# Agent attention and a leaky MLP on one core: scores in two column tiles, another spread of the second batch's side work, another order of loads

## The chip, the core and the metric

The kernel runs on one core of a Trainium2 chip. The metric is the device time of one execution in microseconds (us); three runs of the kernel before took 1022.23, 1023.3 and 1019.7 us, median 1022.23. A separate execution was profiled; its own time is 1020.48 us. Rows of the trace come from that one.

The engines are TensorE (PE in the rows; its weight loads are PEld), VectorE (DVE), ScalarE (ACT), GpSimd (POOL) and SyncE (SP), which issues the loads and stores. Each works through its own instructions in the order in which the program gives them, and waits on semaphores for the others. Products land in PSUM, from which VectorE and ScalarE read.

## The reference

Two batches of 12480 queries, keys and values of 128 channels, and 49 agents per batch. The agents attend to the keys, the queries attend to the agents, and the result goes through a two-layer MLP with a leaky ReLU.

```python
def _attn_ref(q, k, v, agents):
    scale = 1.0 / np.sqrt(q.shape[-1])
    def sm(a, b):
        s = scale * (a @ b.transpose(0, 2, 1))
        s = s - s.max(-1, keepdims=True)
        e = np.exp(s)
        return e / (e.sum(-1, keepdims=True) + 1e-09)
    agent_v = sm(agents, k) @ v
    return (sm(q, agents) @ agent_v).astype(np.float32)

def _moe_ref(x, w_in, w_out):
    h = x @ w_in
    g = np.maximum(0.01 * h, h)
    return (g @ w_out).astype(np.float32)
```

All is float32 but the weights w_in (128 x 2048) and w_out (2048 x 128), which arrive as float64.

## The kernel before

**What is computed where.** For each batch the kernel first finds agent_v (49 x 128) from all keys and values, multiplies it into w_in, and so gets a matrix M of 128 slots x 2048; after that each block of 480 queries needs its softmax over the agents, one product with M (mm1, L681), a ReLU split in a high and a low part (hi on ScalarE L694, lo on VectorE L695), and one product with w_out (mm2, L711). There are 52 blocks, 26 of each batch, and a block has 8 steps; a step is one mm1 (6 passes), one ReLU, and the mm2 of two steps before (12 passes). mm1 writes the PSUM tile h (two buffers), mm2 the tile o.

**Keys and values.** The keys of a batch come in 13 chunks of 8 x 120 keys. k_score (L332) multiplies a chunk by the agents: one product per 120 keys, keys as weights (128 channels x 120 columns), agents as the moving side. For the first batch it moves the agents of both batches at once (w = 2, 98 columns; what the second half writes is written over by the next product, or not read). A float32 product is two passes in the trace, and a pass is one weight load and one matmul. k_copy puts a chunk's scores in s_sb (ScalarE, L359), k_run keeps the running maximum (VectorE, L356). After the last chunk, k_max0 to k_max3 make the maximum per agent. Then a chunk's scores are reduced by it (k_sub), go through exp (k_exp), and are multiplied with the values: in the first batch by k_av32 (L461: weights of 49 columns, the two halves of the array's columns in turn), in the second by k_av2 (L437: values and exponentials split in hi and lo parts by k_vhi, k_vlo, k_ehi and k_elo, the two halves of the rows in turn).

**Start-up.** The first batch's keys, values and the weights have to be through before the first block. Its work is put in order by a planner (class Plan, L18): each piece has an engine, a cost in ns, and the pieces it comes after; the planner simulates the engines and emits what can start first. Where TensorE would idle by its costs, it inserts warm-up products (heat, L827). The loads go out on one queue in the order of the string ORDER (L121: q, k, v, w for the next tile of each), and k, v and w tiles share a ring of LD = 9 buffers, so a load waits until the tile nine before it has been used: a k by run and copy, a v by k_av32, a w by the conversion from float64. That conversion is bits (L236, L237), exp (L245, L246), mant (L304), low (L250), sign (L257), mul (L264). When the last k_av32 is through, f_copy, den (L494), rec, avT, then four products with w_in (mp, L525), m_hi and m_lo make M, and mm1 begins.

**Side work of the second batch.** While the blocks of the first batch run, the second batch's keys and values are worked through beside them. `at(step, fn, ...)` puts a piece at a step; within a step the order is mm1, ReLU, the side pieces in the order of their registration, then mm2. The query softmax of each block is registered first: q_mm, q_x and q_add stand at step 2 of each block, q_tr at 3, p_trans of the block before at 2. The second batch's score chunks stand at step 5 of blocks 0 to 12, k_max0 to k_max3 in block 13, and the 26 half chunks of values (h) are spread from there over U steps; a k_av2 follows each second one by 7 steps. q_mm, k_score of the second batch, the k_max products and k_av2 all write the PSUM tile aux, of which there is one buffer: each waits until the readers of the one before have emptied it.

## Time and profile before

| | |
|---|---|
| three runs | 1022.23, 1023.3, 1019.7 us |
| profiled execution, own time | 1020.48 us |
| its span, first to last instruction | 1018.7 us |
| TensorE busy | 984.0 us (97%) |
| VectorE, ScalarE, GpSimd busy | 734.0, 604.5, 384.7 us |
| mean granted TensorE clock | 0.992 |

The span is the time from the first to the last instruction of the program; the 1.8 us between it and the execution's time lie outside. Busy times add up over stages that have different limits, so they are read by stretch below. The granted clock is the share of the full 2.4 GHz that TensorE got; its lower level is 1.2 GHz, 0.50. The chain of waits is followed back from the last instruction, at each step to what released it.

### The profile page before, as it was taken

How to read it: one execution, taken by the hardware profiler on the slowest of the kernel's cores; microseconds unless marked ns; L12 is line 12 of the kernel's file. 1: busy time of each engine (PE TensorE's matmuls, PEld its weight loads, DVE VectorE, ACT ScalarE, POOL GpSimd, SP SyncE). 2: the span in 40 equal slices, each digit the busy share in tenths (PEclk: the TensorE clock that was granted, in tenths of full speed). 3: DMA queues.
4: the chain of work that ended last, by engine and by line, in shares of the span. 5: the costliest groups of instructions: out<-in, count | busy, mean ns of one | idle time of the engine just before them, and what ended most of it. 6: DMA issues, size and time to landing. Idle time of an engine off the chain costs nothing.

```text
span 1018.7 us, 21488 instructions
## 1 busy us (share of the span) xinstructions
PE 984.0 (97%) x8899; PEld 846.2 (83%) x8899; DVE 734.0 (72%) x1071; ACT 604.5 (59%) x806; POOL 384.7 (38%) x557
## 2 busy tenths in 40 slices
PE   8889999999999999899989999999999999999998
PEld 7757888888887988789878788888888888888886
DVE  7667667677676787679767677777777777777774
ACT  4565565565554665566656566666666666665654
POOL 2103333233232665467555233333333333334320
PEclk9999999999999999899999999999999999999999
DMA  9841112112002113112201001010101010101000
GB/s 343 303 172 37 43 39 79 40 40 79 21 21 79 40 49 90 40 40 82 58 21 40 21 21 40 21 40 21 40 21 41 20 40 21 40 21 40 20 21 20
DMA packets 24028, 57.61 MB, mean 57 GB/s; under 512 B 2787, under 2 KB 16355, under 8 KB 23931
## 3 DMA queue, kind: packets, MB, share of 16 engines
q1 hardware_dynamic: 23787, 56.13, 16.9%
q8 instruction: 69, 1.13, 0.5%
q14 instruction: 28, 0.23, 0.1%
q10 hardware_dynamic: 144, 0.12, 0.0%
HBM read 43.46 MB, written 12.78 MB: 55 GB/s over the span
## 4 chain that ended last, share of the span: by engine, by line
PE 88%; DVE 6%; ACT 3%; DMA 2%; issue 1%; POOL 0%; SPq 0%; POOLq 0%; ACTq 0%; DVEq 0%
PE o L711 50%; PE h L681 26%; PE aux L581 3%; DVE lo L695 3%; PE aux L345 2%; PE o L721 2%; PE sc L345 1%; ACT hi L694 1%; PE aux L437 1%; DMA vt<-in_v_dram 1%; DMA kt<-in_k_dram 1%; PE avw L461 1%; DVE sq L594 0%; DVE pt L657 0%; DVE run L356 0%
## 5 line engine op out<-in xcount | busy, mean ns | idle before, releaser
L695 DVE SCALAR_TENSOR_TENSOR lo<-h,hi 128x960 fp32r<-128x960 f32 x416 | 481.2, 1157 | 247.3 <-ACT hi L694 241.2
L694 ACT ACTIVATE hi<-h 128x960 fp32r<-128x960 f32 x416 | 405.1, 974 | 339.3 <-PE h L681 335.2
L711 PE MATMUL o<-hi,wo_hi 64*128 64x480 f32 x1664 | 367.9, 385 | 0.9 <-ACT oT L732 0.9
L711 PE MATMUL o<-hi,wo_lo 64*128 64x480 f32 x1664 | 359.6, 377 | 0.0
L681 PE MATMUL h<-pT,m_hi 64*128 64x480 f32 x1664 | 294.3, 378 | 1.9 <-DVE lo L695 1.1
L711 PE MATMUL o<-lo,wo_hi 64*128 64x480 f32 x1664 | 293.1, 377 | 0.0
L711 PEld LDWEIGHTS o<-hi,wo_hi 64*128 64x128 f32 x1664 | 212.9, 185 | 33.3 <-ACT oT L732 9.1
L711 PEld LDWEIGHTS o<-hi,wo_lo 64*128 64x128 f32 x1664 | 213.1, 185 | 21.8
L681 PEld LDWEIGHTS h<-pT,m_hi 64*128 64x128 f32 x1664 | 195.2, 185 | 25.8 <-DVE lo L695 2.6
L711 PEld LDWEIGHTS o<-lo,wo_hi 64*128 64x128 f32 x1664 | 196.2, 185 | 22.7
L681 PE MATMUL h<-pT,m_lo 64*128 64x480 f32 x832 | 201.9, 376 | 0.0
L311 POOL TENSOR_TENSOR qlo<-qt,qhi 128x480 fp32r<-128x480 f32 x52 | 63.7, 1225 | 194.8 <-ACT qhi L565 193.1
L681 PEld LDWEIGHTS h<-pT,m_lo 64*128 64x128 f32 x832 | 115.4, 185 | 11.4
L311 POOL TENSOR_TENSOR pT<-pt,pT 128x480 fp32r<-128x480 f32 x52 | 63.4, 1219 | 162.8 <-ACT pT L662 162.8
L650 POOL TENSOR_TENSOR pd<-d,rs 128x375 f32<-128x375 f32 x52 | 43.0, 827 | 83.0 <-DVE rs L645 77.5
L743 POOL TENSOR_TENSOR oT<-oT 128x480 f32<-128x480 f32 x51 | 62.7, 1229 | 10.6 <-ACT oT L732 10.6
L311 POOL TENSOR_TENSOR d<-st,mm 128x375 f32<-128x375 f32 x52 | 43.5, 837 | 50.1 <-DVE mm L616 49.3
L732 ACT COPY oT<-o 128x960 f32<-128x960 f32 x51 | 49.1, 962 | 19.8 <-PE o L711 19.6
L610 POOL COPY sm<-sm 64x15 f32<-64x15 f32 x52 | 10.3, 199 | 82.0 <-DVE sm L630 81.9
L311 POOL TENSOR_TENSOR vr<-vt,vr 120x512 fp32r<-120x512 f32 x26 | 33.7, 1297 | 6.4 <-DVE vr L306 5.5
L657 DVE STREAM_TRANSPOSE pt<-pd 128x480 f32<-128x480 f32 x52 | 34.8, 670 | 0.0
L599 DVE STREAM_TRANSPOSE st<-sq 128x480 f32<-128x480 f32 x52 | 34.8, 669 | 0.0
(130 smaller groups left out, 898.0 us busy)
## 6 DMA issues: line engine op xcount, KB each, us to landing
qt<-in_q_dram SPq DMA_DIRECT2D x53, 240.0 KB, 2.8
kt<-in_k_dram SPq DMA_DIRECT2D x26, 480.0 KB, 6.1
out_dram<-oT SPq DMA_DIRECT2D x51, 240.0 KB, 2.0
vt<-in_v_dram SPq DMA_DIRECT2D x13, 520.0 KB, 6.5
vt<-in_v_dram SPq DMA_DIRECT2D x13, 487.5 KB, 4.8
w<-in_w_in_dram SPq DMA_DIRECT2D x4, 512.0 KB, 6.6
w<-in_w_out_dram SPq DMA_DIRECT2D x4, 512.0 KB, 8.2
out_dram<-oT SPq DMA_DIRECT2D x1, 120.0 KB, 1.7
```

What stands on the lines that cost most here:

```text
L311: eng.tensor_tensor(out=o, in0=x, in1=y, op=ALU.subtract)
L345: nc.tensor.matmul(ps[:TP, j * NA:(j + w) * NA], lhsT=k_t[b, c][:, j, :], rhs=a_sb[:, b:b + w, :].rearrange("p b a -> p (b a)"), start=Tru ...
L581: nc.tensor.matmul(ps[:, g, :NB], lhsT=w[b][r], rhs=x[r], start=(n == 0), stop=(n == 2))
L599: nc.vector.transpose(t.rearrange("p n a -> p (n a)"), s_t[i])
L650: nc.gpsimd.tensor_tensor(out=pd[:, :, :A0], in0=d, in1=w.to_broadcast([P, NT, A0]), op=ALU.mult,)
L657: nc.vector.transpose(t, pd.rearrange("p n a -> p (n a)"))
L681: nc.tensor.matmul(ps[:, g, :NB], lhsT=w[b][r, cols(2 * p + g)], rhs=t[r, x], start=(n == 0), stop=(n == 2),)
L694: nc.scalar.activation(hi, ps, AF.Relu)
L695: nc.vector.scalar_tensor_tensor(out=lo, in0=ps, scalar=0.0, in1=hi.bitcast(F32), op0=ALU.max, op1=ALU.subtract,)
L711: nc.tensor.matmul(o[:, g, :NB], lhsT=w[r], rhs=x[r], start=start, stop=stop)
L732: nc.scalar.copy(t, o[:, :, :NB])
L743: nc.gpsimd.tensor_tensor(out=t[:, 0], in0=t[:, 0], in1=t[:, 1], op=ALU.add)
```

## The change

Three edits. In k_score each product of 128 x 120 weights is made in two, on columns 0 to 63 and 64 to 119 of the array, and the moving side has 49 columns in both batches. The second batch's side work gets another spread: its last three score chunks stand at other steps, so that k_max0 begins at block 11 instead of 13 and the values are spread over U = 100 steps instead of 84. ORDER is another string, and two of the planner's costs change (a half chunk of scores 850 to 480, a half chunk of k_av32 480 to 510).

```diff
-    ORDER = "qkwkkwkkkkkkwwkkkkvvvvvvvvwwwqvvvwvvq"
+    ORDER = "qkwwkkkkkkkwkkkkkwvvvqwvvvvwqvwvvvvvw"
...
     def k_score(b, c, g, pool=None, parts=2):
-        w = 2 if b == 0 else 1
...
         for j in range(g * CH // parts, (g + 1) * CH // parts):
-            nc.tensor.matmul(
-                ps[:TP, j * NA:(j + w) * NA], lhsT=k_t[b, c][:, j, :],
-                rhs=a_sb[:, b:b + w, :].rearrange("p b a -> p (b a)"), start=True, stop=True,
-            )
+            for r in (slice(0, HALF), slice(HALF, TP)):
+                nc.tensor.matmul(
+                    ps[r, j * NA:(j + 1) * NA], lhsT=k_t[b, c][:, j, r], rhs=a_sb[:, b, :],
+                    start=True, stop=True,
+                )
...
         i0 = (b - 1) * BPB
-        n0 = i0 + NCH
+        n0 = i0 + NCH - 2
         for c in range(NCH):
-            s = NP * (i0 + c)
+            s = NP * (i0 + c) + 5 if c < NCH - 3 else NP * n0 - (9, 4, 2)[c - NCH + 3]
             for d in range(c, min(c + 3, NCH)) if c == 0 else (c + 2,) if c + 2 < NCH else ():
-                at(s, load_k, b, d)
-            at(s + 5, k_score, b, c, 0)
-            at(s + 5, k_score, b, c, 1)
-            at(s + 5, k_keep, b, c)
+                at(max(s - 5, 0), load_k, b, d)
+            at(s, k_score, b, c, 0)
+            at(s, k_score, b, c, 1)
+            at(s, k_keep, b, c)
...
         s0, lag = 5, 7
-        U = (BPB - NCH) * NP - NP - s0 - lag
+        U = (BPB - NCH + 2) * NP - NP - s0 - lag
...
-                add(("s", c, g), "pe", 850, k_score, (0, c, g, ps_h), after)
+                add(("s", c, g), "pe", 480, k_score, (0, c, g, ps_h), after)
...
-                add(("av", h), "pe", 480, k_av32, (0, h), [("v", c), ("e", c)] + prev)
+                add(("av", h), "pe", 510, k_av32, (0, h), [("v", c), ("e", c)] + prev)
```

Lines behind k_score are 4 lower in the changed kernel: L437 becomes L433, L581 becomes L577, L681 becomes L677, L711 becomes L707.

What the change makes of TensorE's order at a score chunk of the second batch (block 0, step 5; aux is the PSUM tile, kt the chunk of keys). Before:

```order
L711 MATMUL o<-hi,wo_lo 128x480 x2
L711 MATMUL o<-lo,wo_hi 128x480 x4
L681 MATMUL h<-pT,m_hi_98 128x480 x4
L681 MATMUL h<-pT,m_lo_99 128x480 x2
L345 MATMUL aux<-a_sb,kt 120x49 x8
```

After:

```order
L707 MATMUL o<-lo,wo_hi 128x480 x4
L677 MATMUL h<-pT,m_hi_98 128x480 x4
L677 MATMUL h<-pT,m_lo_99 128x480 x2
L341 MATMUL aux<-a_sb,kt 64x49
L341 MATMUL aux<-a_sb,kt 56x49
```

The eight products of 120 columns became eight pairs, of which the first is shown; they stand at the same place, behind the mm1 of step 5.

TensorE's order around a k_av2 of the second batch. Before, in block 18, where it falls on step 2 (the L581 rows are q_mm):

```order
L681 MATMUL h<-pT,m_hi_98 128x480 x4
L681 MATMUL h<-pT,m_lo_99 128x480 x2
L581 MATMUL aux<-qhi,a_hi_94 128x480 x2
L581 MATMUL aux<-qhi,a_lo_96 128x480 x2
L581 MATMUL aux<-qlo,a_hi_94 128x480 x2
L437 MATMUL aux<-vr_110,er_114 113x258 x8
L437 MATMUL aux<-vr_111,er_115 113x258 x8
L711 MATMUL o<-hi,wo_hi 128x480 x2
```

After, at step 0 of a block:

```order
L677 MATMUL h<-pT,m_hi_98 128x480 x4
L677 MATMUL h<-pT,m_lo_99 128x480 x2
L433 MATMUL aux<-vr_110,er_114 113x258 x8
L433 MATMUL aux<-vr_111,er_115 113x258 x8
L707 MATMUL o<-hi,wo_hi 128x480 x2
```

and two steps on in the same block:

```order
L677 MATMUL h<-pT,m_hi_98 128x480 x4
L677 MATMUL h<-pT,m_lo_99 128x480 x2
L577 MATMUL aux<-qhi,a_hi_94 128x480 x2
L577 MATMUL aux<-qhi,a_lo_96 128x480 x2
L577 MATMUL aux<-qlo,a_hi_94 128x480 x2
L707 MATMUL o<-hi,wo_hi 128x480 x2
```

Each of the 13 k_av2 stands at step 0 of a block now, from block 13 to block 25; before they stood at steps 7, 6, 4, 3, 2, 0, 7, 6, 5, 3, 2, 1 and 0 of blocks 14 to 25.

VectorE's order at the end of the start-up, around den. Before (w_628 is the last w tile, followed by two v tiles in the order of loads; w_533 and w_548 are earlier ones):

```order
L250 SCALAR_TENSOR_TENSOR w_out_sb<-w_533,w_out_sb 128x512
L264 TENSOR_TENSOR w_in_sb<-w_in_sb,e 128x512
L264 TENSOR_TENSOR w_out_sb<-w_out_sb,e 128x512
L257 SCALAR_TENSOR_TENSOR e<-w_628,e 128x512
L494 TENSOR_SCALAR den<-aux 128x1
L496 RECIPROCAL rec<-den 128x1
L250 SCALAR_TENSOR_TENSOR w_out_sb<-w_628,w_out_sb 128x512
L264 TENSOR_TENSOR w_out_sb<-w_out_sb,e 128x512
L550 SCALAR_TENSOR_TENSOR m_lo_99<-mp,rec,m_hi_98 128x512 x4
```

After (w_803 is the last of all the loads of the start-up):

```order
L236 TENSOR_SCALAR em<-w_803 128x512
L237 TENSOR_SCALAR e<-w_803 128x512
L490 TENSOR_SCALAR den<-aux 128x1
L492 RECIPROCAL rec<-den 128x1
L257 SCALAR_TENSOR_TENSOR e<-w_803,e 128x512
L546 SCALAR_TENSOR_TENSOR m_lo_99<-mp,rec,m_hi_98 128x512
L250 SCALAR_TENSOR_TENSOR w_out_sb<-w_803,w_out_sb 128x512
L546 SCALAR_TENSOR_TENSOR m_lo_99<-mp,rec,m_hi_98 128x512
L264 TENSOR_TENSOR w_out_sb<-w_out_sb,e 128x512
L546 SCALAR_TENSOR_TENSOR m_lo_99<-mp,rec,m_hi_98 128x512 x2
```

The first step of the last w tile's conversion (L236, L237) now stands just ahead of den, and the rest of it among the m_lo.

## Rows read from the trace of the kernel before

**Rows 1.** The page: busy time, share of the span and instructions of each engine, and the chain that ended last by engine.

```profile
PE 984.0 (97%) x8899; PEld 846.2 (83%) x8899; DVE 734.0 (72%) x1071; ACT 604.5 (59%) x806; POOL 384.7 (38%) x557
PE 88%; DVE 6%; ACT 3%; DMA 2%; issue 1%; POOL 0%; SPq 0%; POOLq 0%; ACTq 0%; DVEq 0%
```

**Rows 2.** Busy time by stretch (from:to in us, its length, then each engine's busy us and instructions, granted clock, share of the DMA engines, GB/s): the start-up up to the first ReLU; the value stage, blocks 13 to 25; a score block (block 3); a plain block (block 27). Blocks are cut at their first ReLU.

```profile
0.00:70.90 70.90, 58.97 (x520) 50.51 (x520) 47.57 (x112) 39.55 (x73) 10.01 (x30) 0.98 0.79 294
317.10:576.10 259.00, 243.34 (x2220) 213.03 (x2218) 193.59 (x288) 152.91 (x218) 145.32 (x187) 0.98 0.17 49
128.80:147.60 18.80, 18.80 (x171) 16.38 (x171) 13.00 (x19) 10.95 (x14) 6.04 (x9) 1.00 0.17 53
592.90:609.70 16.80, 16.80 (x157) 14.37 (x155) 12.49 (x18) 10.48 (x14) 6.08 (x10) 1.00 0.10 30
```

**Rows 3.** The chain of waits: start us, us, what, and how many passes. Scores of the first batch (98 moving columns), products of 128 x 128 with 128 moving columns (L294), k_av32 (L461), an mm2, scores of the second batch (49 moving columns), k_av2 (L437).

```profile
16.05 5.28 PE sc L345 x48
...
37.24 0.90 PE avw L294 x8
...
40.04 7.26 PE avw L461 x128
...
97.67 1.31 PE o L711 x12
...
101.60 1.81 PE aux L345 x16
...
367.48 0.96 PE aux L437 x16
```

**Rows 4.** Busy time by stretch, columns as in rows 2: blocks 17, 18, 19, 22, 23 and 24.

```profile
390.70:409.60 18.90, 17.93 (x171) 15.70 (x169) 13.80 (x22) 11.29 (x18) 12.16 (x17) 1.00 0.19 54
409.60:433.50 23.90, 20.76 (x177) 17.95 (x175) 15.95 (x23) 11.68 (x17) 10.86 (x15) 0.86 0.14 42
433.50:452.10 18.60, 18.60 (x186) 16.14 (x184) 14.69 (x24) 11.72 (x19) 12.99 (x16) 1.00 0.19 54
487.70:506.60 18.90, 17.95 (x171) 15.70 (x169) 13.81 (x22) 11.37 (x17) 12.18 (x17) 1.00 0.20 54
506.60:529.50 22.90, 19.77 (x173) 17.33 (x172) 16.25 (x23) 11.71 (x17) 11.14 (x15) 0.93 0.07 23
529.50:548.40 18.90, 18.14 (x178) 17.49 (x177) 14.27 (x20) 12.98 (x21) 13.33 (x17) 1.00 0.09 27
```

**Rows 5.** The chain of waits in block 18, at its step 2 (L594 is q_add).

```profile
416.66 0.55 DVE sq L594
...
417.25 2.06 PE aux L437 x11
419.31 2.40 PE o L711 x12
```

**Rows 6.** The chain of waits at steps 0 and 2 of block 19.

```profile
432.62 0.56 PE h L681 x6
433.18 0.93 PE aux L437 x14
...
437.51 0.65 PE h L681 x6
438.16 0.65 PE aux L581 x6
```

**Rows 7.** Groups of instructions in the first 105 us: line, engine, operation, tiles, shapes, count, busy us, mean ns of one, idle time before them and what ended it.

```profile
L356 DVE TENSOR_TENSOR run<-sc,run 120x392 f32<-120x392 f32 x12 | 6.8, 565 | 4.3 <-ACT s_sb L359 2.2 <-PE sc L345 1.1 <-ACT e L245 0.9
...
L246 ACT ACTIVATE e<-e,off 128x512 int32<-128x512 int32 x8 | 5.8, 722 | 0.3
...
L257 DVE SCALAR_TENSOR_TENSOR e<-w,e 128x512 int32<-128x512 int32 x8 | 5.4, 679 | 1.6 <-ACT e L246 1.6
...
L237 DVE TENSOR_SCALAR e<-w 128x512 int32<-128x512 int32 x8 | 3.4, 422 | 0.0
```

**Rows 8.** Weight loads of the scores and of k_av32: count, shortest, median and longest in ns, first and last start, rows x columns.

```profile
L345 PEld LDWEIGHTS sc<-a_sb,kt x152: 179/185/185, 16.0 to 34.6; 128*120 128x120 f32 x152
...
L461 PEld LDWEIGHTS avw<-vt,s_sb x208: 120/124/208, 40.0 to 57.6; 120*49 120x49 f32 x104
```

**Rows 9.** The chain of waits in the start-up: the first scores, the last running maximum, the last value tile, den.

```profile
11.53 1.08 PE sc L345 x8
...
35.31 0.58 DVE run L356
...
47.31 9.44 DMA vt<-in_v_dram
...
59.59 0.17 DVE den L494
```

**Rows 10.** Busy time by stretch in the start-up, columns as in rows 2.

```profile
0.00:24.00 24.00, 21.50 (x153) 19.20 (x153) 16.73 (x50) 11.06 (x19) 6.23 (x26) 1.00 0.91 340
40.00:48.00 8.00, 7.27 (x129) 7.01 (x128) 6.07 (x14) 5.62 (x12) 0.00 (x0) 1.00 0.71 213
48.00:56.00 8.00, 4.93 (x56) 4.57 (x58) 5.46 (x12) 7.12 (x12) 1.20 (x1) 0.79 1.02 411
0.00:59.60 59.60, 50.31 (x477) 45.55 (x478) 42.62 (x104) 34.39 (x62) 10.01 (x30) 0.97 0.91 336
```

**Rows 11.** What the load queue waited for: us in total, times, longest (L211 loads a tile of w_out).

```profile
SPq L211 <- PE avw L461: 6.2, 2, 5.7
```

## The prediction

> **What bounds the kernel now.** I read the page first, then busy time by stretch, then the chain of waits inside the stretches that stand out. TensorE is busy 97% of the span and carries 88% of the chain that ended last, so a microsecond taken from it is a microsecond of the span, except in the start-up [rows 1]. A plain block of the second half takes 16.8 us with TensorE busy throughout; one that also scores a chunk of the second batch takes 18.8, so a chunk costs 2.0 us, of which 1.81 are its 16 matrix passes [rows 2, 3]. The start-up lasts 70.9 us with TensorE busy 59.0 and loads at 294 GB/s on average [rows 2]. Between the two lies the value stage, blocks 13 to 25, 259.0 us instead of 13 x 16.8 = 218.4 [rows 2]. Its k_av2 costs 0.9 us where nothing is in its way: the block from 433.5 us has two and takes 18.6. So a block with one should take 17.7. Five do not: 18.9, 23.9, 18.9, 22.9 and 18.9 [rows 4]. Together 103.5 - 5 x 17.7 = 15.0 us are lost there.
>
> **The value stage.** Where those five lose time is fixed by the step at which k_av2 is placed. Before, it stands at 12 + 84h//25 steps after the 104th, h odd, which in those blocks is step 3, 2, 3, 2 and 1 of the block. q_mm is always at step 2, and both write aux, of which there is one buffer. The chain shows the dearest case: k_av2 stands behind q_mm on TensorE and starts only when VectorE's q_add (L594) has emptied aux, at 417.25; what is behind it, all of mm2 and mm1, waits too. The granted clock of that block is 0.86, and its twelve mm2 passes take 2.40 us, where they take 1.31 at the full 2.4 GHz: TensorE had stood idle, fell to the lower level, and paid again [rows 3 to 5]. After, the formula is 12 + 100h//25 = 12 + 4h, for odd h always step 0, one per block in blocks 13 to 25. In the block from 433.5 us one k_av2 stands at step 0: it starts right behind mm1, and the next q_mm two steps later starts behind its mm1 too, with no piece of waiting between [rows 6]. All five losses go, -15.0. The whole stage works at the same amount over more steps; the fullest block now keeps VectorE 14.7 and GpSimd 13.0 of 18.6 us [rows 4], so neither becomes the bound. Against it: the k_max sequence only moves from block 13 to 11 and keeps its length, and three score chunks move to steps 7, 4 and 6, two steps apart, where each waits until ScalarE and VectorE have emptied the aux of the last. Two steps are about 4 us, and VectorE's run, the longer of the two, takes 0.57 [rows 7], so I leave 1 us for it. Bounds: -15, and 0 if each of 12 blocks pays the 1.2 us that a k_av2 at step 3 pays now. I take -14.
>
> **The score passes in column halves.** Each chunk was 8 products of 2 passes, 16 passes, and becomes 32, on 64 and 56 columns in turn. The trace has no 64-column load of 128 rows. What a pass costs now: 110 ns with 98 moving columns (5.28 us for 48), 113 with 49 (1.81 for 16) [rows 3]. Half the stream changed nothing, so it is the weight load that sets it. Loads take 185 ns with 120 columns and 124 with 49 [rows 8], which is 61/71 = 0.86 ns a column: about 103 for 120, 52 for a half. Whether two halves load side by side decides everything. If they do not, a pair costs 104 and 32 passes 1.7 to 1.9 us, no gain. If they do, a pair costs about 55 to 60 and 32 passes 0.88 to 0.96. Two rows bear on it. k_av32 (L461) already alternates column halves with full rows: 57 ns a pass (7.26 us for 128), while a stream of 128 columns alone takes 112 (0.90 for 8) [rows 3]. So the halves do run their streams side by side; its loads of 42 ns would have fitted in 57 either way. And k_av2 (L437) alternates row halves with loads of 113 columns, about 97 ns by the slope: 60 ns a pass (0.96 for 16) [rows 3]. There loads do overlap between two parts of the array. I take side by side at 30 ns a pass: 0.96 instead of 1.81, -0.85 a chunk, on the path for 13 chunks: -11. Bounds: -12 (27.5 ns a pass) and, with loads and streams of the halves one after another, +16, worked out below.
>
> The Trainium skill ("TensorE: Matmul & The Clock Gate", Part 3) says that a weight load overlaps matmuls in flight only when the row groups differ; the two halves here have the same rows. Its page "TensorEngine Tiling (Array Packing)", Key Properties, says that different tiles load and multiply in parallel. By the first the sum would be that of the third rival below (1040), by the second that of this forecast (991); k_av32's 57 ns a pass, in the same rows, agrees with the second.
>
> **The start-up.** Scores run from 11.5 to 35 us now, 13 x 16 passes x 110 ns = 22.9 us and with few gaps; the last run (L356) ends at 35.9, the first k_av32 starts at 40.04, the last value tile is waited for until 56.75, den (L494) comes at 59.59 and the first ReLU at 70.9 [rows 2, 3, 9]. In between SyncE's queue stands: the loads are in a ring of nine, a w load waits 5.7 us for the first k_av32, and in 40 to 48 us the DMAs move 213 GB/s instead of 411 [rows 10, 11]. At 30 ns a pass the scores need 12.5 us of TensorE and follow the loads: the first 24 us bring 340 x 24 = 8.2 MB [rows 10], and agents, one q, 13 k and 3 w are 8.3 MB. VectorE then sets the pace, its order holding 13 run (565 ns each) and the conversion of three w tiles ahead of the last run; I put that at 29.5 us and the first k_av32, 4.1 us later as now plus two conversion steps of 0.68, at 35 [rows 7]. The load that waits for it (again the 27th of the ring) no longer stands. All 18.3 MB then land at 24 + 10.1/0.411 = 48.6 us. Last of these is now a w, not a value tile, and VectorE's order has its first step (L236 and L237, 0.42 us each) ahead of den. That gives den at 51 to 52 if VectorE keeps up: it did 42.6 us of work up to 59.6 [rows 10], and needs 0.7 less. It has to run nearly full from 8 us on, so I take 52, 7.5 earlier. After den this w still costs two activations (0.72 each) and a VectorE pass of 0.68 that now lie ahead of it [rows 7], 2.1 us, of which something hides behind the products (mp) that follow den: +1.5. Start-up -6; bounds -9 and +1 (the planner puts 30 warm-up passes behind the first 14 instead of 9, free only where TensorE is idle).
>
> **Sum.** The profiled execution takes 1020.5 us, 1018.7 of it span. 1020.5 - 14 - 11 - 6 = 989.5. The median of the three runs, 1022.2, stands 1.7 above this execution; on that scale 991.
>
> **Rivals.**
> (1) The halves load one after another, as fast as a whole: no gain in the scores. The start-up then keeps its pace (0, the w at the end and the extra warm-up cancelling the value tile's earlier landing). 1020.5 - 14 = 1006.5, 1008 on the median's scale. For it: 110 against 113 ns shows a bound by loads, and 52 + 52 is the same 104. Against it: k_av2's 60 ns.
> (2) The tiles pay, but the regular pattern of the value stage costs something in every block: each k_av2 delays q_mm through its two adds on VectorE, or k_vhi now always falls on step 2, beside q_add and p_trans. 12 x 1.2 = 14.4 eats the gain: 1003.5, so 1005. Against it: the two step-0 cases of the trace pay nothing.
> (3) Slower: each half's load waits for the stream of the other half in the same rows. 52 + 49 x 0.87 (112 ns for 128 columns [rows 3]) = 95 ns a pass, 3.04 us a chunk, +1.23 on each of 26 chunks, all on TensorE's path: 1020.5 - 14 + 32 = 1038.5, so 1040. It turns the whole change from 73 ns a pass on (14/26 = 0.54 us a chunk more than 1.81). Against it: k_av32 would then take 42 + 113 = 155 ns a pass and takes 57.
> (4) The change not doing what it says can't be: the rows of the order show the halves and every k_av2 at step 0.
>
> **Chances.** The forecast 62%, (1) 19%, (2) 10%, (3) 5%, and 4% for what I priced too low on several parts at once. The forecast's own range is 984 (all bounds at their best: 1020.5 - 15 - 12 - 9 = 984.5, 986 on the median's scale, and a little) to 999; to leave no more than 2 in 10 out it has to reach over (2) and (1): 984 to 1009. A measurement of this kernel tells 0.3%, 3 us, from no change. Faster by more than that: all but (3) and most of the last case, 0.91; same 0.03; slower 0.06.
>
> **What would show it.** Score blocks of the second batch at 18.0 us instead of 18.8, the score passes at about 0.96 us for 32; at 18.8, (1) holds, at 20, (3). Blocks 13 to 24 all near 17.7 with a granted clock of 1.00 and no wait of L433 for q_add; 18.9 in each would be (2). The first ReLU near 65 instead of 70.9, with 40 to 48 us at about 400 GB/s; if VectorE still waits or den stays near 59, the start-up's term is wrong. The forecast as a whole is wrong if the score passes come out above 57 ns.

## The result and the profile after

The changed kernel takes 991.36 us, median of four runs (991.17 to 991.6); the kernel before takes 1022.54, median of four. The ratio is 0.97, 95% interval 0.9681 to 0.9719: 31 us less. The forecast was 991, with the range 984 to 1009. The profiled execution takes 991.27 us, its span is 989.5, which is 29.2 less than before.

The page of the changed kernel answers to [rows 1]: busy time of each engine, and the chain that ended last by engine.

```profile
PE 965.1 (98%) x9336; PEld 826.8 (84%) x9336; DVE 726.5 (73%) x1071; ACT 602.9 (61%) x806; POOL 386.8 (39%) x557
...
PE 91%; DVE 4%; DMA 2%; ACT 1%; issue 1%; SPq 0%; POOL 0%; POOLq 0%; ACTq 0%
```

TensorE has 18.9 us less to do, although it runs 437 instructions more, and waits less: VectorE's share of the chain falls from 6% to 4%, ScalarE's from 3% to 1%. TensorE itself now carries 91% of the chain.

Busy time by stretch, columns as in [rows 2]: the start-up; blocks 0 to 10; blocks 11 to 25; a score block; block 10, which has two chunks; blocks 17 and 18; block 25.

```profile
0.00:65.80 65.80, 55.30 (x749) 43.21 (x749) 48.69 (x112) 39.06 (x72) 11.18 (x30) 1.00 0.83 317
65.80:268.60 202.80, 200.90 (x2086) 169.32 (x2088) 146.51 (x207) 121.69 (x159) 67.17 (x102) 1.00 0.16 50
268.60:546.90 278.30, 271.55 (x2528) 236.06 (x2526) 211.08 (x322) 173.01 (x245) 157.60 (x205) 1.00 0.17 49
121.50:139.50 18.00, 18.00 (x187) 15.32 (x185) 12.86 (x19) 10.93 (x14) 6.00 (x9) 1.00 0.17 56
249.20:268.60 19.40, 19.40 (x222) 16.38 (x222) 13.23 (x19) 11.36 (x16) 4.89 (x9) 1.00 0.19 54
376.90:394.70 17.80, 17.80 (x173) 15.67 (x172) 13.80 (x21) 11.35 (x18) 10.85 (x15) 1.00 0.19 57
394.70:412.40 17.70, 17.70 (x173) 15.67 (x171) 13.79 (x21) 11.23 (x17) 10.73 (x15) 1.00 0.21 58
519.10:546.90 27.80, 23.49 (x186) 17.75 (x184) 17.33 (x29) 13.68 (x21) 7.52 (x12) 1.00 0.06 19
```

The same two stretches of blocks of the kernel before:

```profile
70.90:279.40 208.50, 206.60 (x1844) 176.59 (x1846) 146.37 (x205) 120.88 (x156) 66.89 (x101) 1.00 0.14 46
279.40:576.10 296.70, 281.04 (x2558) 245.28 (x2558) 219.72 (x324) 174.82 (x246) 157.48 (x205) 0.98 0.17 48
```

From these the 29.2 us are divided. The start-up gives 70.9 - 65.8 = 5.1. A block with one chunk takes 18.07 on average instead of 18.82, and a plain block 16.78 in both, so a chunk costs 1.29 over a plain block instead of 2.04, or 0.76 less when the averages aren't rounded first: 13 x 0.76 = 9.9. In blocks 11 to 25 the kernel before also held two chunks, 296.7 - 2 x 2.04 = 292.6, and the kernel after holds none there: 292.6 - 278.3 = 14.3. The sum is 29.3, which is the 29.2 of the spans but for rounding.

Blocks 17 and 18 answer to the first two of [rows 4], 18.9 and 23.9 us. TensorE is now busy in all of both, at the full clock, and so it is in every block from 13 to 24 (17.75 to 17.87 us). The chain of waits at steps 0 and 2 of block 17 reads as that of [rows 6], for a block that is one of five like it:

```profile
375.98 0.56 PE h L677 x5
376.54 0.91 PE aux L433 x14
...
380.85 0.65 PE h L677 x6
381.50 0.65 PE aux L577 x6
```

A score chunk in the chain, beside 1.81 for 16 in [rows 3]. Below it are the weight loads of that chunk, and of the chunk of [rows 3] in the kernel before (columns as in [rows 8]):

```profile
149.99 1.06 PE aux L341 x30
```

```profile
L341 PEld LDWEIGHTS aux<-a_sb,kt x32: 126/132/138, 149.9 to 150.8; 128*64 128x64 f32 x16, 128*56 128x56 f32 x16
```

```profile
L345 PEld LDWEIGHTS aux<-a_sb,kt x16: 179/185/185, 101.5 to 103.1; 128*120 128x120 f32 x16
```

1.06 us are 33 ns for each of 32 passes (the chain puts two of them elsewhere), but no pass runs at that pace. The starts of the single loads show two rows of 16 at the same time: on the columns from 0 on a load of 64 columns starts every 58 ns, on those from 64 on one of 56 columns every 52 ns. Before, a load of 120 columns starts every 105 ns. The loads are recorded with 138, 132 and 185 ns, some 80 ns more than these distances: the duration of one doesn't say how fast they follow each other.

The chain of the start-up, answering to [rows 9]:

```profile
31.49 0.47 DVE run L352
...
38.24 6.13 PE avw L457 x109
44.37 8.31 DMA vt<-in_v_dram
...
55.94 1.89 PE mp L521 x4
...
65.82 0.98 ACT hi L690
```

The last running maximum ends at 31.96 instead of 35.89, the first k_av32 starts at 38.24 instead of 40.04, the last value tile is there at 52.68 instead of 56.75, den starts at 55.8 instead of 59.59.

### The profile page after: what moved, and what is told of

It is laid out like the page before. It is cut to its first block, busy times and chain, and to the rows that moved or that the text cites. A ratio compares the mean times of both kernels' runs of the same rounds, so it can differ in the third digit from the quotient of the medians.

```text
span 989.5 us, 22385 instructions
## 1 busy us (share of the span) xinstructions
PE 965.1 (98%) x9336; PEld 826.8 (84%) x9336; DVE 726.5 (73%) x1071; ACT 602.9 (61%) x806; POOL 386.8 (39%) x557
## 4 chain that ended last, share of the span: by engine, by line
PE 91%; DVE 4%; DMA 2%; ACT 1%; issue 1%; SPq 0%; POOL 0%; POOLq 0%; ACTq 0%
PE o L707 54%; PE h L677 27%; PE aux L577 3%; PE o L717 2%; DVE lo L691 1%; PE aux L341 1%; PE aux L433 1%; DMA kt<-in_k_dram 1%; PE sc L341 1%; DMA vt<-in_v_dram 1%; PE avw L457 1%; ACT hi L690 1%; DVE run L352 0%; PE avw L294 0%; PE mp L521 0%
## 5 line engine op out<-in xcount | busy, mean ns | idle before, releaser
L707 PE MATMUL o<-hi,wo_hi 64*128 64x480 f32 x1664 | 365.8, 384 | 0.8 <-ACT oT L728 0.8
L707 PE MATMUL o<-hi,wo_lo 64*128 64x480 f32 x1664 | 357.2, 376 | 0.0
L677 PE MATMUL h<-pT,m_hi 64*128 64x480 f32 x1664 | 292.5, 377 | 1.9 <-DVE lo L691 1.1
L707 PE MATMUL o<-lo,wo_hi 64*128 64x480 f32 x1664 | 291.3, 376 | 0.0
L707 PEld LDWEIGHTS o<-hi,wo_hi 64*128 64x128 f32 x1664 | 210.4, 184 | 33.4 <-ACT oT L728 9.5
L707 PEld LDWEIGHTS o<-hi,wo_lo 64*128 64x128 f32 x1664 | 211.0, 184 | 21.5
L677 PEld LDWEIGHTS h<-pT,m_hi 64*128 64x128 f32 x1664 | 194.0, 184 | 25.6 <-DVE lo L691 2.6
L707 PEld LDWEIGHTS o<-lo,wo_hi 64*128 64x128 f32 x1664 | 195.0, 184 | 22.4
L677 PE MATMUL h<-pT,m_lo 64*128 64x480 f32 x832 | 200.7, 376 | 0.0
L311 POOL TENSOR_TENSOR qlo<-qt,qhi 128x480 fp32r<-128x480 f32 x52 | 64.4, 1238 | 168.2 <-ACT qhi L561 168.2
L677 PEld LDWEIGHTS h<-pT,m_lo 64*128 64x128 f32 x832 | 114.4, 184 | 11.2
```

Of the source, the lines that this page charges most:

```text
L311: eng.tensor_tensor(out=o, in0=x, in1=y, op=ALU.subtract)
L677: nc.tensor.matmul(ps[:, g, :NB], lhsT=w[b][r, cols(2 * p + g)], rhs=t[r, x], start=(n == 0), stop=(n == 2),)
L707: nc.tensor.matmul(o[:, g, :NB], lhsT=w[r], rhs=x[r], start=start, stop=stop)
```

## The experiments

All ratios are against the kernel before on the same chip, with the 95% interval.

### One part alone: e1, e2 and e7

e1 is the kernel before with the column halves only; the string of loads, the planner's costs and the spread are the old ones.

```diff
-        w = 2 if b == 0 else 1
...
+            for r in (slice(0, HALF), slice(HALF, TP)):
+                nc.tensor.matmul(
+                    ps[r, j * NA:(j + 1) * NA], lhsT=k_t[b, c][:, j, r], rhs=a_sb[:, b, :],
+                    start=True, stop=True,
+                )
```

> The kernel before with the score passes in column halves alone (spread, order of loads and planner costs as before). Theory (three terms that add up): each of the 13 score chunks of the second batch costs 0.76 us less, -10; the start-up gains little because the order of loads and the costs are the old ones, 0 to -3; the value stage keeps its 15 us of losses. 1009 to 1012 us. Rival (the tiles pay only with the other two edits, since the time saved in the score blocks comes back as waiting elsewhere): above 1016 us.

Measured: 1008.86 us, ratio 0.9871 (0.985 to 0.9891), span 1005.7. Score blocks take 18.07 us, as in the changed kernel, and the five blocks keep their losses (18.9, 22.9, 18.9, 22.9, 18.9). The first ReLU comes at 68.7, with a mean clock of 0.95 up to it. Of the 13.0 us in the span, 9.8 are the chunks, 2.2 the start-up, and 1.0 block 18, which took 23.9 before. So the scores' term belongs to the tiles, and the start-up's only in part.

e2 is the kernel before with the new spread only.

```diff
-        n0 = i0 + NCH
+        n0 = i0 + NCH - 2
...
-            s = NP * (i0 + c)
+            s = NP * (i0 + c) + 5 if c < NCH - 3 else NP * n0 - (9, 4, 2)[c - NCH + 3]
...
-        U = (BPB - NCH) * NP - NP - s0 - lag
+        U = (BPB - NCH + 2) * NP - NP - s0 - lag
```

> The kernel before with the new spread of the second batch's scores and values alone, passes of 120 columns. Theory: the value stage loses its 15 us of waits, three score chunks of 2.0 us each move to other steps at no cost: -14, 1008 us, with blocks 13 to 24 near 17.8 us each and a first ReLU at 70.9 as before. Rival (the longer passes collide with q_mm at the new steps): -10 or less, 1012 us or more.

Measured: 1007.44 us, ratio 0.986 (0.9832 to 0.9888), span 1005.6. Blocks 13 to 24 take 17.76 to 17.87 us, score blocks 18.83, the first ReLU comes at 70.5. Block 25:

```profile
534.20:563.70 29.50, 24.94 (x181) 18.63 (x179) 17.59 (x29) 13.66 (x20) 7.50 (x11) 0.94 0.06 17
```

The spread alone takes the five losses away; 1.7 us of it go again in block 25 (27.8 in the changed kernel), where the clock stands at the lower level from 556.4 to 559.8.

e7 leaves the kernel before as it is, and moves only the k_av2 that stand at steps 1 to 3 (blocks 17, 18, 22, 23 and 24) to step 4 of the same block.

```diff
-                at(s + lag, k_av2, b, h // 2)
+                t = s + lag
+                t += (4 - t % NP) if t % NP in (1, 2, 3) and h < NH - 1 else 0
+                at(t, k_av2, b, h // 2)
```

> The kernel before with one edit: the five k_av2 that stand at step 1, 2 or 3 of a block (blocks 17, 18, 22, 23, 24) move to step 4 of the same block; the values are still spread over 84 steps. Theory (the place of k_av2 against q_mm costs the 15 us, not how dense the values are): these five blocks fall to about 17.8 us, -14 to -15, 1008 us. Rival (the values are spread too densely over 84 steps, and 100 steps cure it): the waits come back at other places, 1015 us or more.

Measured: 1007.33 us, ratio 0.9853 (0.9833 to 0.9873), span 1005.6. Blocks 17 and 18 (18.9 and 23.9 before):

```profile
390.60:408.30 17.70, 17.70 (x171) 15.84 (x169) 13.84 (x22) 11.29 (x17) 12.10 (x17) 1.00 0.21 58
408.30:426.30 18.00, 18.00 (x180) 15.89 (x178) 15.97 (x23) 11.74 (x18) 10.98 (x15) 1.00 0.20 56
```

Block 18 still has 15.97 us of work for VectorE, where the changed kernel's has 13.79, and takes 18.0 us all the same. It is the step of k_av2, not how densely the value work is spread, that cost the 15 us; the longer spread is one way among others to get k_av2 away from steps 1 to 3.

### The place of k_av2 turned against itself: e6

The changed kernel, with every k_av2 of blocks 13 to 24 two steps later, at step 2, beside q_mm.

```diff
-                at(s + lag, k_av2, b, h // 2)
+                at(s + lag + (2 if h < NH - 1 else 0), k_av2, b, h // 2)
```

> The changed kernel with each k_av2 of blocks 13 to 24 two steps later, so at step 2, where q_mm stands; still one per block over 100 steps. Theory (q_mm and the one aux buffer make the cost): every one of the 12 blocks pays what blocks 18 and 23 paid before, 5 to 6 us, with TensorE falling to half its clock in each or some: +60 to +74, 1051 to 1065 us; at the least +3 a block, 1027 us. Rival (the spread over 100 steps gives the engines room and the place does not matter): 991 to 995 us.

Measured: 1051.31 us, ratio 1.0293 (1.0266 to 1.032). Two such blocks by stretch, the first of the twelve and a later one, and the chain of the later one at step 2:

```profile
305.20:326.10 20.90, 17.95 (x173) 15.51 (x171) 13.99 (x21) 11.26 (x17) 10.71 (x15) 1.00 0.17 48
393.30:416.90 23.60, 20.66 (x171) 17.91 (x169) 13.99 (x21) 11.26 (x17) 10.68 (x15) 0.86 0.15 43
```

```profile
399.93 0.55 DVE sq L590
...
400.52 2.06 PE aux L433 x15
402.59 2.40 PE o L707 x12
```

These are the three rows of [rows 5] over again: TensorE waits for q_add (named sq here), then works at the lower level, 2.06 instead of 0.91 and 2.40 instead of 1.31. The wait comes in all twelve blocks. The first of them keeps the full clock and takes 20.9 us, 3.1 more than its 17.8 in the changed kernel, for the wait alone; the clock falls in the eleven others, which take 22.2 to 23.8. The same work two steps further on costs 60 us, 5 for each k_av2.

### Why a half pass is short: e5, e12, e8 and e9

In e5 each half chunk goes through the four products of one column half first and then through the four of the other, so that the halves take turns only every eight passes.

```diff
-        for j in range(g * CH // parts, (g + 1) * CH // parts):
-            for r in (slice(0, HALF), slice(HALF, TP)):
+        for r in (slice(0, HALF), slice(HALF, TP)):
+            for j in range(g * CH // parts, (g + 1) * CH // parts):
```

> The changed kernel, but of each half chunk first the four products of columns 0 to 63, then the four of columns 64 to 119, so that neighbours in the order mostly use the same half of the array. Theory (it pays because the loads of two different halves run side by side): the passes go back to 52 to 57 ns each, 32 of them take about 1.7 to 1.8 us, score blocks 18.8 us instead of 18.07, +10 in the second batch and 0 to +4 in the start-up: 1001 to 1005 us. Rival (a load of half the columns is cheaper whatever stands beside it): 1.06 us for 32 passes as in the changed kernel, 991 us.

Measured: 997.94 us, ratio 0.9765 (0.9735 to 0.9795). The chunk in the chain:

```profile
151.92 1.34 PE aux L341 x31
```

```profile
L341 PEld LDWEIGHTS aux<-a_sb,kt x11: 126/138/138, 151.8 to 152.2; 128*64 128x64 f32 x8, 128*56 128x56 f32 x3
```

1.34 us for 32 passes are 42 ns for each, neither the 33 of the rival nor the 52 or more of the theory. It is a mean of two paces. The second row shows the loads of the first half chunk up to 152.25 us: three loads of the second half start before the eighth and last of the first. So TensorE does not keep to the order of the program here: it begins the passes of the other columns while those of the first columns are still to come, and the edit takes away only part of the overlap. Within a half nothing changes. A load of 64 columns starts every 58 ns and one of 56 columns every 52 ns, as in the changed kernel, whether the other half is loading at that time (from 152.12 on) or not (until then). The two halves load side by side and don't slow each other; one after the other they would take 16 x 58 + 16 x 52 = 1.76 us.

e12 has the changed kernel move 98 columns instead of 49 in three of four products of the second batch (what falls on the neighbour's place is written over by the next product).

```diff
-        for j in range(g * CH // parts, (g + 1) * CH // parts):
+        for j in reversed(range(g * CH // parts, (g + 1) * CH // parts)):
...
+                w = 2 if b and j % (CH // parts) else 1
...
-                    ps[r, j * NA:(j + 1) * NA], lhsT=k_t[b, c][:, j, r], rhs=a_sb[:, b, :],
+                    ps[r, (j + 1 - w) * NA:(j + 1) * NA], lhsT=k_t[b, c][:, j, r],
+                    rhs=a_sb[:, b + 1 - w:b + 1, :].rearrange("p b a -> p (b a)"),
```

> The changed kernel with 98 moving columns instead of 49 in three of four score products of the second batch (the agents of both batches; what the other batch's columns write is written over by the next product). Theory (the loads of the halves set the 66 ns of a pair): 32 passes stay at 1.06 us, 991 us. Rival (the streams set it; the halves out of turn took 42 ns a pass, near the 43 of a 49-column stream): with 98 columns a stream takes 85 ns, two side by side in at least 85, so 24 passes at 43 to 60 and 8 at 33: 1.3 to 1.7 us, +3 to +8, 994 to 999 us.

Measured in one execution: 995.44 us. The chunk in the chain:

```profile
151.42 1.37 PE aux L342 x25
```

In both halves the loads of the passes with 98 columns start every 84 ns, at the same times. That is the stream: 98 x 0.87 = 85 (by the 112 ns for 128 columns of [rows 3]). With 49 columns the stream is 43 and the load of 64 or 56 columns, 58 or 52, sets the pace; with 98 the stream is the longer and sets it. A half has 12 passes of 98 columns and 4 of 49 in a chunk: 12 x 84 + 4 x 58 = 1240 ns, and 130 at the ends of the chunk, as below, give the 1.37. With whole loads the stream made no difference, since the 105 of the load are more than either.

e8 uses four column tiles of 32, 32, 32 and 24 in both batches, e9 in the second batch only.

```diff
-            for r in (slice(0, HALF), slice(HALF, TP)):
+            w = HALF if b == 0 else SL
+            for r in [slice(o, min(o + w, TP)) for o in range(0, TP, w)]:
...
-                    start=True, stop=True,
+                    start=True, stop=True, tile_position=(0, r.start),
```

This is e9's; e8 has a width of 32 (SL) in both batches. Lines behind k_score are one higher in e8, e9 and e11, and two in e12.

> The changed kernel with each score product in four column tiles of 32 (the last 24) instead of two: 64 passes a chunk. Theory (the load of a tile's own columns sets the pace and tiles load side by side): four passes take as long as the longest of a 32-column load (28 ns) and a 49-column stream (43 ns), so a chunk 0.7 us instead of 1.06, 986 to 988 us. Rival (33 ns is what TensorE needs for any pass): 64 x 33 = 2.1 us a chunk, +1.05 x 13 = +14 in the second batch and more in the start-up, 1005 to 1015 us.

> The changed kernel with four column tiles of 32 in the second batch's scores alone; the start-up is untouched. Theory (the quarters' 64 passes take 0.82 us beside mm1 and mm2, as the trace with quarters everywhere shows, and that trace lost its time in the start-up alone): score blocks 17.84 instead of 18.07 us, 13 x 0.24 = -3.1: 988.3 us, first ReLU at 65.8. Rival (what the scores gain comes back as waiting in the next stage): 991 us.

Measured: e8 1001.27 us, ratio 0.9803 (0.9775 to 0.9831); e9 987.57 (986.97 to 988.1), ratio 0.9676 (0.9658 to 0.9694). The interval of e9 overlaps that of the changed kernel, and the kernel before ran 2.4 us faster beside e9; the traces tell the two apart, with a span of 986.3 instead of 989.5. The chunk in e9's chain, and its loads:

```profile
166.80 0.83 PE aux L342 x59
```

```profile
L342 PEld LDWEIGHTS aux<-a_sb,kt x64: 100/110/110, 166.7 to 167.4; 128*32 128x32 f32 x48, 128*24 128x24 f32 x16
```

All four tiles start a load within some 20 ns, and each of them the next one 43 ns later. That is the stream of 49 columns; a load of 32 columns is 28 by the slope of [rows 8]. A score block takes 17.83 us, 0.24 less than in the changed kernel, and 13 x 0.24 = 3.1 is all but 0.1 of the difference of the spans.

One rule now covers all five cases: on its own columns a pass takes the longer of its load and its stream, and tiles of different columns work at the same time. The distances are read from the starts of the single loads of one chunk in each trace; the load is an estimate at 0.86 ns a column, by [rows 8], the stream one at 0.87.

| | columns of a tile | moving columns | load, stream (ns) | from load to load (ns) |
|---|---|---|---|---|
| before, second batch | 120 | 49 | 103, 43 | 105 |
| before, first batch | 120 | 98 | 103, 85 | 105 |
| after | 64 and 56 | 49 | 55 and 48, 43 | 58 and 52 |
| e12 | 64 and 56 | 98 | 55 and 48, 85 | 84 |
| e9 | 32 and 24 | 49 | 28 and 21, 43 | 43 |

A chunk of the second batch is 16 times the distance of its widest tile and 0.13 us at its two ends: 16 x 105 + 130 = 1810 ns before, 16 x 58 + 130 = 1058 in the changed kernel, 16 x 43 + 130 = 818 in e9; the chains show 1.81, 1.06 and 0.82 to 0.83.

e8 gains the same in the score blocks, and loses it with more in its start-up:

```profile
0.00:78.40 78.40, 58.94 (x1165) 45.45 (x1165) 48.29 (x112) 39.10 (x72) 11.00 (x30) 0.89 0.74 267
16.00:32.00 16.00, 11.55 (x419) 9.41 (x422) 8.18 (x16) 4.96 (x10) 1.39 (x3) 0.68 0.78 275
```

```profile
PE sc L342 <- issue: 10.0, 5, 3.3
```

The last row is what TensorE waited for before its scores: 10.0 us in five stops in the midst of chunks, the longest 3.3, and "issue" means that nothing which the profile shows held it up. The scores of no other run wait like this. Each stop ends 1.3 to 1.5 us after a 16 KB transfer on the queue of kind "instruction" has landed (in the first, from 13.46 to 16.80, the transfer runs from 14.5 to 15.5), so TensorE seems to have waited for its own code: it goes through 832 short passes of the first batch's scores instead of 416. The chain holds all five. Behind the first of them the clock is at the lower level from 17.0 to 27.2, and twice more later; the last score pass starts at 43.0 us instead of 30.7, and the first ReLU comes 12.6 us later. With halves in the first batch (e9) the 12.6 us are back. How the 2.6 beyond the stops divide between the clock and the order of work was not separated.

### The start-up: e3, e4, e10 and e11

e3 is the changed kernel with the old string of loads, e4 with the planner's two old costs.

```diff
-    ORDER = "qkwwkkkkkkkwkkkkkwvvvqwvvvvwqvwvvvvvw"
+    ORDER = "qkwkkwkkkkkkwwkkkkvvvvvvvvwwwqvvvwvvq"
```

```diff
-                add(("s", c, g), "pe", 480, k_score, (0, c, g, ps_h), after)
+                add(("s", c, g), "pe", 850, k_score, (0, c, g, ps_h), after)
...
-                add(("av", h), "pe", 510, k_av32, (0, h), [("v", c), ("e", c)] + prev)
+                add(("av", h), "pe", 480, k_av32, (0, h), [("v", c), ("e", c)] + prev)
```

> The changed kernel with the old order of loads; tiles, spread and planner costs as changed. Only the start-up can differ. Theory (the order of loads carries part of the start-up's gain, since a w instead of two value tiles lands last and value tiles land earlier): first ReLU 1.5 to 4 us later than the changed kernel's 65.8, 993 to 995 us. Rival (the start-up gains by the shorter score passes alone): 65.8 and 991.4 us within 0.5.

> The changed kernel with the planner's old costs for a half chunk of scores (850) and of k_av32 (480). Only the start-up can differ: the planner believes TensorE busier, so it inserts fewer warm-up products and places conversion steps of w earlier or later. Theory: the passes themselves set the pace, the costs move the first ReLU by at most 1 us from 65.8: 990.5 to 992.5 us. Rival (the plan is what turns the shorter passes into an earlier end): the start-up goes back by 2 to 5 us, 993.5 to 996 us.

Measured: e3 998.07 us (996.28 to 1000.25), ratio 0.9773 (0.975 to 0.9795); e4 998.53 (996.18 to 1002.63), ratio 0.9779 (0.974 to 0.9818). Each by itself costs more than the whole start-up's term, and more than was expected. Their first ReLU comes at 72.7 and 73.8, later than before the change. First e3, 8 to 16 us; then e4, 24 to 40 and 56 to 64 us:

```profile
8.00:16.00 8.00, 5.47 (x81) 4.76 (x78) 4.50 (x10) 3.67 (x7) 0.00 (x0) 0.70 1.02 407
```

```profile
24.00:40.00 16.00, 13.05 (x190) 11.61 (x185) 12.54 (x25) 10.04 (x19) 3.46 (x3) 0.79 0.96 366
56.00:64.00 8.00, 5.30 (x11) 3.30 (x12) 2.68 (x7) 3.01 (x6) 0.00 (x0) 0.61 0.55 221
```

Both have stretches at the lower level; the changed kernel's start-up has a mean clock of 1.00. In e4 there is also another plan: with 850 for a half chunk the planner counts TensorE as busier and puts 20 warm-up passes behind the first 14 instead of 30. And ScalarE's order differs; its chain behind the last value product:

```profile
56.50 0.73 ACT e L245
57.26 0.72 ACT e L246
57.98 0.52 ACT w_out_sb L304
58.50 0.16 ACT avs L466
...
61.63 3.40 PE mp L521 x4
```

f_copy (avs) stands behind three activations of the last w tile, and the four products with w_in take 3.40 us, at the lower level, instead of 1.89. That leads to e10: the changed kernel without the 30 later warm-up passes.

```diff
-            for i in range(n if ("wmm", NM - 1) not in plan.done else 0):
+            for i in range(n if start else 0):
```

> The changed kernel with only the first 14 warm-up products; the 30 that the planner puts into TensorE's idle times are left out, the rest of every engine's order is the same. Theory (the start-up gains because TensorE is kept at its full clock in the gaps that shorter score passes leave): the granted clock falls to 0.50 for one or more stretches before the first ReLU, which comes 3 to 8 us later than 65.8: 994.5 to 999.5 us. Rival (the gain is the order of the conversion steps and loads, the clock does not matter there): within 1 us of 991.4, or earlier.

Measured in two runs: 990.55 and 995.53 us, ratio 0.973 (0.9691 to 0.9769). In the profiled execution the first ReLU comes at 68.7:

```profile
8.00:24.00 16.00, 11.99 (x251) 10.80 (x247) 11.19 (x23) 8.30 (x15) 0.70 (x2) 0.79 1.02 409
32.00:48.00 16.00, 10.77 (x139) 10.09 (x137) 15.54 (x34) 13.07 (x26) 3.12 (x4) 0.79 0.77 259
```

TensorE falls to the lower level twice (12.7 to 19.6, and 36.6 to 43.5) in stretches where it does less. That is 2.9 us, a little under what was expected; but the other run is as fast as the changed kernel, so what the warm-up is worth differs by execution, and two runs don't settle its mean.

e11 goes on from e9: two pieces of VectorE's work (the last step of one w tile's conversion and p_trans) are held back until the second chunk of k_sub is through, so that the first k_av32 comes earlier.

```diff
-            add(("mul", n), "dve", 600, conv_mul, (n, dve), [("low", n), ("sign", n)])
+            add(("mul", n), "dve", 600, conv_mul, (n, dve), [("low", n), ("sign", n)] + [("sub", 1)] * (n == 3))
...
-            add(("chain", n), eng, cost, fn, (0,), [last])
+            add(("chain", n), eng, cost, fn, (0,), [last] + [("sub", 1)] * (fn is p_trans))
```

> The kernel with quarters in the second batch, and in the start-up the last step of the fourth w tile's conversion (L264), its 8 products (L294) and p_trans held back until the second k_sub. Theory (the load that waits for the first k_av32 is issued at 39.3 us, 1.5 us of that because these pieces stand ahead of the first k_sub and k_av32; the value tiles behind it set den): first k_av32 at about 36.7 instead of 38.2, den and the first ReLU 1 to 1.5 us earlier, 987 us. Rival (VectorE, full from 32 to 48 us, sets den, so the held-back pieces come back later): first ReLU at 65.8 or later, 988.3 us or more.

Measured: 987.37 us (986.59 to 987.51), ratio 0.9675 (0.9654 to 0.9696). In the trace the first k_av32 starts at 36.9, den at 54.4, the first ReLU at 64.4, 1.4 us earlier, and the span is 984.8 instead of e9's 986.3. The medians of the two are 0.2 us apart and their runs overlap, so the gain is seen in the profiled executions and not told apart in the times.

## Why the prediction was right, and where it was not

**The total** came out within 0.4 us of the forecast, and that is partly luck. The three terms gave 14.3 for 14, 9.9 for 11 and 5.1 for 6, so on the scale of the profiled executions 29.2 came out for 31: 991.27 instead of 989.5. The forecast was then raised by 1.7, by which the median of the kernel before stood above its profiled execution. The four runs of the changed kernel lie within 0.4 us of its profiled one, so nothing of that kind came back, and the 1.7 made up for what the terms were short of.

**The value stage, 14 forecast, 14.3 found, and shown.** Where k_av2 stands decides: e2 and e7 take the loss away by two different edits, e6 brings it back fourfold (60 against 15). Rival (2), that the regular pattern costs something in each block, is out: the twelve blocks take 17.75 to 17.87 us, and no row of L433 names a wait. The chunks that moved closer cost nothing either: block 10 with two of them takes 19.4, and 16.78 + 2 x 1.29 = 19.36.

**The scores, 11 forecast, 9.9 found: the mechanism as forecast, the size a little off.** "Half the stream changed nothing, so it is the weight load that sets it" holds: whole passes follow each other every 105 ns with 49 and with 98 moving columns. It carries over to halves of 49 moving columns (58 and 52 ns, the load); it would not have with 98, where the stream is the longer (84, e12). "Whether two halves load side by side decides everything" holds too, and they do: e5 doesn't speak against it, since the trace shows the halves side by side there as well for much of the time. The estimate of 52 ns for a half's load, by the slope of the recorded durations, was near: a half of 60 columns would lie between the 52 and 58 of 56 and 64. A pair goes at the pace of the wider half, 58 ns, within the 55 to 60 forecast, so 16 pairs take 0.93 us. What was left out are the 0.13 us at the ends of a chunk: they are in the 1.81 that the sum starts from and not in the 0.96, and so a chunk gained 0.75 instead of 0.85.

Rival (1) falls because the loads of the two halves run at the same time, 58 and 52 ns apart, not by the price of a single one. Rival (3) needed 95 ns a pass, load and stream one after another.

The Trainium skill ("TensorE: Matmul & The Clock Gate", Part 3) lets a load overlap running matmuls only where the row groups differ; by that rule passes of the same rows would cost their load and their stream, the 95 ns of rival (3). In the first passes of e5 rows and columns are the same from pass to pass and they follow every 58 ns, and in the changed kernel the rows are, with 58 and 52 ns; both speak against it for these loads. The other page of the Trainium skill weighed ("TensorEngine Tiling (Array Packing)", Key Properties), by which different tiles load and multiply in parallel, agrees with the two halves at 58 and 52 ns side by side, and with e9's four tiles at 43.

**The start-up, 6 forecast, 5.1 found, by steps that were off in both directions.** That the scores would follow the loads, with VectorE setting the pace, put the last run at 29.5; it ended at 31.96. What the scores waited for, from the rows of L341 up to 60 us (us, times):

```profile
its engine sat idle before it (us, times) until:
  DVE run L352: 7.0, 8
```

The products wait for the running maximum to empty their PSUM tile, and the maximum for them; VectorE is busy 6.04 of the 8 us from 24 on, so it set the pace by its place in a round, not by being full. That the load which waits for the first k_av32 "no longer stands" failed: the queue's waits and the stretches that [rows 10] showed as 213 GB/s in 40 to 48 us are now

```profile
SPq L189 <- PE avw L457: 4.9, 5, 3.2
SPq L211 <- DVE mb L390: 4.0, 1, 4.0
```

```profile
32.00:40.00 8.00, 7.29 (x61) 5.38 (x61) 7.89 (x18) 5.53 (x12) 2.59 (x2) 1.00 0.81 312
40.00:48.00 8.00, 7.29 (x120) 6.47 (x117) 8.00 (x18) 7.64 (x15) 0.00 (x0) 1.00 0.94 318
```

The queue stands 4.0 us for VectorE up to 35.2, and then still 3.2 us for the first k_av32 up to 39.3 (5.7 before), and the 16 us from 32 on lose (411 - 315) / 411 x 16 = 3.7 us of full loading. So the last w landed at 54.0 instead of 48.6, and den came at 55.8 instead of 52. VectorE, meanwhile, is busy in 15.9 of these 16 us. The other error went the other way: den to the first ReLU was to cost 1.5 more for the last w's conversion, 12.8 us, and took 10.0 instead of the 11.3 before. That 3.8 too late and 2.8 too much nearly cancelled is luck. ScalarE's timeline shows the two activations:

```profile
55.67 0.72 ACT L245 ACTIVATE e<-e,off 128x512 int32<-128x512 int32 x1
56.43 0.72 ACT L246 ACTIVATE e<-e,off 128x512 int32<-128x512 int32 x1
57.85 0.69 ACT L542 ACTIVATE m_hi<-mp,rec 128x512 fp32r<-128x512 f32 x1 [0.70 <-PE mp L521]
```

They lie in the time of the mp, and ScalarE still waits 0.70 for it: "of which something hides" should have been all. The prediction also gave the tiles as the cause of this gain, the order of loads as the reason for another last tile, and the costs as the reason for more warm-up. The runs show more than that: tiles alone give 2.2 (e1), and with either of the other two left old the start-up is longer than before (e3, e4), so the three edits don't add up term by term there. TensorE's clock, full all through in the changed kernel, was not among the terms at all; how much of e3's and e4's loss is the clock and how much the other order of work was not separated.

## What to carry to other kernels

A product with few moving columns that is cut into column tiles gets cheaper for as long as its load is longer than its stream, here from 105 to 58 to 43 ns per 120 columns, of which the last is the stream. Take the price of a pass from the distance between loads on the same columns, at two stream lengths. The recorded duration of a load (138 ns at 58) misleads, and so does a chunk's time divided by its passes: 33 and 42 ns were means over two tiles that work at the same time. Where one PSUM buffer is shared, look at the step at which each writer stands before spreading the work: five badly placed products cost 15 us, and twelve cost 60. After shortening TensorE's passes in a stretch that loads or another engine bound, read its waits on "issue" and the granted clock there first: with the shorter passes of e8 the start-up grew by 12.6 us, 10.0 of them stops on "issue".

## What the runs showed of the hardware that was not expected

Passes on one column tile follow each other at the longer of load and stream, every 105 ns with 120 columns, 58 with 64, 52 with 56, at 49 moving columns; 84 with 98 moving columns; 43 with 32 or 24 columns. Tiles of different columns with the same rows do this at the same time, and where the program gives one tile eight passes before the other (e5), TensorE doesn't wait for them to begin the other's. Where the load sets the distance, its recorded duration is some 80 ns longer: 185, 138 and 132 for 105, 58 and 52. The slope of the durations, 0.86 ns a column, is a fair price, and the durations themselves are not.

Scores in quarters stopped five times in the start-up of e8, for 10.0 us in all, each time until 1.3 to 1.5 us after a transfer of kind "instruction" had landed; the same quarters between mm1 and mm2 (e9) never did. That it was the code they waited for is read from this regularity; no run took it away.

Block 25, the second batch's matrix stage, has two lengths whatever the edit: 27.7 to 27.8 us in the kernel before, the changed kernel, e9 and e11, and 29.3 to 29.5 in e2, e5, e7 and e10, each time with the clock at the lower level once. Part of what e2, e5 and e7 were short of their sums is this.
